# A shifted DMA copy and one mask in the decoding of the second layer's weights, with a load two steps sooner

## The chip, the cores and the metric

The kernel runs on one core of a Trainium2 chip. The metric is the device time of one execution in microseconds (us): the median of three runs. The profile is that of one further execution, whose own time stands beside its span.

## The reference

```python
w = softmax over the 7 taps of weight[8, 7], one set per group of 24 channels
x = causal convolution of x[4, 4096, 192] with w, along the sequence
x = x.reshape(16384, 192)
g = np.maximum(x @ moe_w_in, 0.0) ** 2        # 192 x 2048
x = g @ moe_w_out                             # 2048 x 192
h = x @ moe2_w_in
out = np.maximum(0.01 * h, h) @ moe2_w_out
```

The weights of both layers are float64. In DRAM each value is two 32-bit words, and the kernel decodes them on the chip.

## The kernel before

**Tiles and steps.** Tokens go in 32 tiles of 512. Each layer has 2048 hidden channels, which are handled in eight pieces p = 0 to 7 of 256; a unit (layer, tile) takes eight steps, one per piece. In a step PE computes the piece's hidden values of one tile (`g1`: h, nine rounds of products) and, two steps behind (LAG), adds the products with w_out of an earlier piece into the output banks (`g2` for the first two tiles, which are worked as a pair; `g2_one` with `paired` for all others). ACT takes h through the activation and rounds it to its high part (hi), the DVE subtracts to get the low part (lo). Steps 0 to 15 are the pair (1,0), (1,1); steps 16 to 23 are (1,2); 24 to 31 (1,3); from 32 on come (2,0), (2,1) and so on. Layer 2's piece p is first used in step 32 + p.

**Weights.** `load_w` (L166 to L172) issues five DMAs on SP per piece. Loads are numbered 0 to 15: load 8 + p is layer 2's piece p. The tile of 128 x 768 pairs of words stands in a place that is lent to it until its own weights come there (`lent`), or in a stage tile "w" or "y". `decode` makes the high and the low part of a piece p in steps on the DVE, some handed to ACT:

- mantissa: m = the high word's lowest 9 bits (L234); rest: the low word times 2^-32 plus m, written over the low word (L250). Together they are the fraction below the high part.
- exponent: t = the high word's exponent and upper mantissa bits (L266), and on ACT a relu that rescales it (L269).
- sign: puts the sign into t (L281); then four DMA copies on SP put the high parts where the products read them (L287).
- power: p = t's power of two (L296); low: low word times p times a power of two (L302, three instructions of one or two blocks).

**What sets the order.** The scheduler keeps the program's order on each engine. In steps 0 to 15 a hand-written string per step (ROW, played by `play`) says what comes when: d the next decode operation, L the next load, p a part of the convolution, a letter each for activation, square, high and low part. From step 16 on `single` and `fill` choose by a model of the engines' times (`clock`, `on`): a decode operation is placed if its gate allows it and if the model says that the step's own chain still ends in time. A load is issued after the low part of the piece whose place it takes (AFTER).

**POOL.** Its queue holds the casts of x by DMA, the accumulating copies of layer 1's decoding (L245), the later `differences` (L149, L151), and one more thing: where two halves of the PE array change over on an output bank, PE's new product depends on an empty instruction on POOL, which depends on PE's last product of the other half. For `g2` these are the 16 at L670, for `paired` those at L718:

```python
                if holder.get((u, k), half) != half:
                    done = nc.gpsimd.nop(nofuse=True).ins
                    tc.add_manual_dep(done, lastly[u, k].name, in_turn, reason="halves take turns on a bank")
                    tc.add_manual_dep(ins, done.name, in_turn, reason="halves take turns on a bank")
```

Of the kernel before, what the change touches and what calls it, by code (L numbers as in the profile page):

```python
# [8 lines left out]

F32 = mybir.dt.float32  # L10
F32R = mybir.dt.float32r
I32 = mybir.dt.int32
U32 = mybir.dt.uint32
ACTF = mybir.ActivationFunctionType
ALU = mybir.AluOpType
# [3 lines left out]
P = 128  # L19
TT = 512  # L20
# [16 lines left out]
BY_DMA = 3  # L37
ADD = 3
CAST = ((1, 2), (1, 3))
ASIDE = (2, 3, 4)  # L40

# [9 lines left out]
    "AdbaBwyddwHdp",  # L53
    "ddgAbpdahllB",
    "ybpdwLAyBdpawThrp",
    "ldppABabhlp",
    "AyBydpabhdww",
    "lyAdappLhlBdwp",
    "pAbpayhBrbywd",
    "wddBAlahlrdb",  # L60
)
# [5 lines left out]
def conv_moe_moe2_kernel(  # L67
# [10 lines left out]
    nc = tc.nc  # L78
    B, S, D = x.shape
# [4 lines left out]
    NP = NF // 2  # L84
# [6 lines left out]
    NW = NI + NO  # L91

    const = ctx.enter_context(tc.tile_pool(name="const", bufs=1))
    stage = ctx.enter_context(tc.tile_pool(name="stage", bufs=1))
# [9 lines left out]
    f32 = lambda ap: ap.bitcast(F32)  # L104
# [9 lines left out]
    WIDE = NI + 21 * R  # L114
# [44 lines left out]
    ring = const.tile([P, 3, TT], F32, name="ring")  # L159

    def load_w(l, p, t):
# [9 lines left out]
        nc.sync.dma_start(out=to[:, :, 2 * R:], in_=src[:, :, 0:2 * P])  # L171
        nc.sync.dma_start(out=to[:, :, 0:2 * R], in_=src[:, :, 2 * P:])  # L172

    held, holding = deque(), [False]
    ready, owner_m, raised_at, signed = {}, {}, {}, {}

    clock = {"D": 0, "A": 0}
# [22 lines left out]
    def decode(l, p, t, a, b):  # L200

        lo_w, hi_w = t[:, a:b, 0], t[:, a:b, 1]
        n = b - a
        one, two = 160 + n * 52 // 100, 170 + n * 104 // 100
# [17 lines left out]
            lows.append((lambda s: s[:, NO - a:], z[:, WI_LO:WI_LO + NI]))  # L222
        T = {}
        by_add = l == 1 and p >= ADD

        def mantissa():
            if by_add and p % 2:
# [26 lines left out]
        def exponent():  # L254
            release()
            if l == 1 and p > 0:
                if "t" not in words:
                    words["t"] = lent(0)
                T["t"] = words["t"][:, p % 2 * NW:(p % 2 + 1) * NW]
            elif l == 2 and p in ASIDE:  # L260
                if "t2" not in words:
                    words["t2"] = stage.tile([P, NW, 2], I32, tag="y", name="t2").rearrange("p n w -> p (n w)")
                T["t"] = words["t2"][:, p % 2 * NW:(p % 2 + 1) * NW]
            else:
                T["t"] = stage.tile([P, NW], I32, tag="t", name="t")[:, 0:n]
            nc.vector.tensor_scalar(out=T["t"], in0=hi_w, scalar1=0x7FFFFE00, scalar2=None, op0=ALU.bitwise_and)  # L266

            def relu():
                nc.scalar.activation(out=T["t"], in_=T["t"], func=ACTF.Relu, scale=8.0, bias=bias_e)  # L269
                raised_at[l, p] = max(clock["A"], clock["D"] + AFTER_D) + 870 + AFTER_A  # L270

            on_scalar(relu, 850)
# [19 lines left out]
        def power():  # L292
            if not (l == 1 and p > 0):
                owner_m["m"] = 0
            T["p"] = stage.tile([P, NW], I32, tag="t" if l == 1 and p > 0 else "m", name="p")[:, 0:n]
            nc.vector.tensor_scalar(out=T["p"], in0=T["t"], scalar1=-(2 ** 23), scalar2=None, op0=ALU.bitwise_and)  # L296

        def low_():
            assert not by_add or "added" in T
            ready[l, p, 1] = True  # L300
            for of, to in lows:
                nc.vector.scalar_tensor_tensor(  # L302
                    out=to, in0=of(T["r"]) if by_add else f32(of(lo_w)), scalar=2.0 ** -20, in1=f32(of(T["p"])), op0=ALU.mult, op1=ALU.mult
                )

        return [(one, mantissa), (two, rest)], [(one, exponent)], [(two, sign), (one, power), (two, low_)]


    phases = [[(1, 0), (1, 1)], [(1, 2)], [(1, 3)], [(2, 0)], [(2, 1)], [(2, 2)], [(2, 3)]]
# [531 lines left out]
    def evac(u):  # L841

        l, q = u
        o = ops.pop(u)
        tags.extend(tag_of[u][k] for k in ((0, "m"), (1, "m"), (0, "r"), (1, "r")))
        T = [2 * q, 2 * q + 1]
        z = {}

        def take(i):
            z[i] = ring[:, i, :]  # L850
            (nc.vector.tensor_copy if i else nc.scalar.copy)(out=z[i], in_=o[i, "m"])

        def shift(i):
            if i == 0:
                z["s"], z["r"] = f32(stage.tile([P, NW], I32, tag="m", name="zs")[:, 0:TT]), ring[:, 2, :]
            nc.scalar.copy(out=z["s"][halves(i)], in_=o[i, "r"][halves(1 - i)])

        def add(i):
            v = halves(i)
            nc.vector.tensor_add(out=z["r"][v], in0=o[i, "r"][v], in1=z["s"][v])  # L860

        now = [lambda: take(0), lambda: take(1), lambda: shift(0), lambda: add(0), lambda: shift(1), lambda: add(1)]
        if l == 1:
            then = []
            for i in range(2):
                b, a = splits((2, T[i]), lambda i=i: z[i], lambda: z["r"])
                then += [p + ((2, T[i]),) for p in ((a[0], b[0], a[1], b[1]) if i else a + b)]
            return now, then

        y = y_of(2 * q)  # L870

        def main(i):
            nc.vector.transpose(out=y()[:, i], in_=z[i])
            for j in range(4):
                store(y(), i, j, T[i], 32 * j)

        def rest():
            nc.vector.transpose(out=y()[:, 2], in_=z["r"])
            for j in range(4):
                store(y(), 2, j, T[j // 2], P + 32 * (j % 2))  # L880

        return now, [(700, lambda: main(0), None, None), (700, lambda: main(1), None, None), (700, rest, None, None)]

    with tc.manual_schedule():
# [7 lines left out]
        def load(n):  # L892
            if n >= len(loads):
                return
            l, p = loads[n]
            since[n] = now[0]
            if n < NP or NP + 1 < n < 2 * NP - 1:
                t = lent(n if n < NP else n + 1 - NP).rearrange("p (c w) -> p c w", w=2)
            else:
                t = stage.tile([P, NW, 2], I32, tag="w" if n == NP + 1 else "y", name="w")  # L900
            load_w(l, p, t)
            words[n] = t

        def fill_dec():
            parts = [(0, NO, NW), (0, 0, NO)] + [(n, 0, NW) for n in range(1, len(loads))]
# [7 lines left out]
            def stage_(j, k):  # L913
                if j >= len(parts):
                    return
                n, a, b = parts[j]
                cost = {0: (780, 1180), 1: (620,), 2: (1230, 580, 1260)}
                l, p = loads[n]
                need = first_use["w", l, p] - LEAD_W - (((2 if p >= ADD else 3), 1, 0) if l == 1 else (4, 2, 1))[k]
                for m, c in enumerate(cost[k]):  # L920
                    def run(j=j, k=k, m=m, n=n):
                        if j not in got:
                            begin(j)
                        got[j][k][m][1]()
                    run.second = (k, m) in ((0, 1), (2, 2))
                    gate = (lambda n=n: now[0] >= since[n] + 2) if k == 0 and m == 0 else None
                    if l == 2 and (k, m) == (2, 0):
                        gate = lambda p=p: (2, p) in raised_at and raised_at[2, p] <= clock["D"]
                    if l == 2 and k == 1 and p:
                        at_ = p - 2 if p in ASIDE[1:] else ASIDE[0] - 1 if p == ASIDE[-1] + 1 else p - 1  # L930
                        gate = lambda at_=at_: (p == ASIDE[0] or signed[2, at_] + 5000 <= clock["D"]) and not (
                            SECOND <= now[0] < THIRD and now[0] % NP == NP - 1
                        )
                    dec.append((need + (LATE and l == 1 and p >= ADD and (k, m) == (2, 2)) + (l == 2 and k == 2 and m > 0), c, run, gate))
                if k == 2 and a == 0:
                    if n in AFTER:
                        dec.append((need, 0, lambda n=n: load(AFTER[n]), None))

            stage_(0, 1)
            stage_(0, 0)  # L940
            for j in range(len(parts)):
                if parts[j][0] == NP - 1 or j == 0:
                    stage_(j, 2)
                    stage_(j + 1, 0)
                    stage_(j + 1, 1)
                else:
                    stage_(j + 1, 0)
                    early = j + 1 < len(parts) and parts[j + 1][0] - NP in ASIDE + (ASIDE[-1] + 1,)
                    if early:
                        stage_(j + 1, 1)  # L950
                    stage_(j, 2)
                    if not early:
                        stage_(j + 1, 1)
            for k in range(len(dec) - 2, -1, -1):
                dec[k] = (min(dec[k][0], dec[k + 1][0]),) + dec[k][1:]
            for k, z in enumerate(dec):
# [285 lines left out]
        for s in range(NS):  # L1242
# [62 lines left out]
                    decode_one()  # L1305
            begun += length(s - 1)
            if s == 2 * NP:
                clock["D"] = clock["A"] = begun + 2500
            if late:
                if late[0] not in hi:  # L1310
# [48 lines left out]
```

## Time and profile before

| | |
|---|---|
| median of three runs | 2041.4 us (2041.13 to 2041.49) |
| profiled execution | 2040.87 us |
| its span | 2039.2 us |
| granted TensorE clock | 1.0 |
| busy: PE, PEld, DVE, ACT, POOL | 2030.6, 1964.9, 1698.7, 1458.2, 42.2 us |

The span is what the trace covers; the execution's own time is 1.7 us longer. PE is TensorE's matmuls and PEld its weight loads. A releaser in square brackets is the instruction whose end let the waiting engine go on. An engine's name with a q (POOLq, SPq) is its queue: there stand the waits, DMA issues and empty instructions, which are not counted as busy.

### The profile page before, as it was taken

How to read it: one execution, taken by the hardware profiler on the slowest of the kernel's cores; microseconds unless marked ns; L12 is line 12 of the kernel's file. 1: busy time of each engine (PE TensorE's matmuls, PEld its weight loads, DVE VectorE, ACT ScalarE, POOL GpSimd, SP SyncE). 2: the span in 40 equal slices, each digit the busy share in tenths (PEclk: the TensorE clock that was granted, in tenths of full speed). 3: DMA queues.
4: the chain of work that ended last, by engine and by line, in shares of the span. 5: the costliest groups of instructions: out<-in, count | busy, mean ns of one | idle time of the engine just before them, and what ended most of it. 6: DMA issues, size and time to landing. Idle time of an engine off the chain costs nothing.

```text
span 2039.2 us, 47094 instructions
## 1 busy us (share of the span) xinstructions
PE 2030.6 (100%) x18552; PEld 1964.9 (96%) x18552; DVE 1698.7 (83%) x2656; ACT 1458.2 (72%) x2638; POOL 42.2 (2%) x82
## 2 busy tenths in 40 slices
PE   9999999999999999999999999999999999999998
PEld 5999999999999999999999999999999999999998
DVE  8899878788887978879788897888878888798775
ACT  7897567676676866767677676766767667687675
POOL 1004010000000000000000000000000000000000
PEclk9999999999999999999999999999999999999999
DMA  8662121222212212131211212122122221221111
GB/s 189 146 160 75 25 45 27 49 30 49 38 27 52 37 44 36 30 60 30 48 26 39 52 27 48 29 50 38 27 49 30 49 38 27 52 35 42 24 30 27
DMA packets 240087, 98.66 MB, mean 48 GB/s; under 512 B 208568, under 2 KB 225080, under 8 KB 239864
## 3 DMA queue, kind: packets, MB, share of 16 engines
q1 hardware_dynamic: 236696, 92.54, 22.7%
q0 software_dynamic: 1168, 2.75, 0.7%
q8 instruction: 145, 2.38, 0.5%
q14 instruction: 78, 0.64, 0.1%
q10 hardware_dynamic: 2000, 0.36, 0.1%
HBM read 25.19 MB, written 12.58 MB: 19 GB/s over the span
## 4 chain that ended last, share of the span: by engine, by line
PE 98%; ACT 1%; DVE 0%; DMA 0%; issue 0%; POOL 0%; DVEq 0%; ACTq 0%; POOLq 0%
PE h L556 48%; PE o1m L556 16%; PE o1r L556 16%; PE o0m L556 8%; PE o0r L556 8%; PE conv L460 1%; PE idle_o L1003 0%; ACT g L588 0%; DMA w<-lent 0%; ACT g L597 0%; ACT hi L615 0%; DVE lo L619 0%; DVE w L302 0%; ACT x L487 0%; ACT ring L241 0%
## 5 line engine op out<-in xcount | busy, mean ns | idle before, releaser
L556 PE MATMUL h<-x,w 64*128 64x512 f32 x9216 | 1350.9, 376 | 0.5 <-DMA w<-lent 0.4
L556 PEld LDWEIGHTS h<-x,w 64*128 64x128 f32 x9216 | 1061.5, 186 | 7.3 <-ACT hi L615 0.8
L619 DVE TENSOR_TENSOR lo<-g,hi 128x512 fp32r<-128x512 f32 x1022 | 665.6, 689 | 266.2 <-ACT hi L615 250.6
L556 PE MATMUL o1m<-hi,w 64*128 64x512 f32 x2044 | 613.8, 378 | 0.3 <-ACT ring L755 0.3
L615 ACT CAST hi<-g 128x512 fp32r<-128x512 f32 x1020 | 586.1, 621 | 22.9 <-DVE g L595 12.9
L556 PE MATMUL o1r<-hi,w 64*128 64x512 f32 x2012 | 601.0, 378 | 0.0
L590 ACT ACTIVATE g<-h 128x512 f32<-128x512 f32 x512 | 281.7, 596 | 308.3 <-PE h L556 308.3
L588 ACT ACTIVATE g<-h 128x512 f32<-128x512 f32 x512 | 282.8, 596 | 159.8 <-PE h L556 159.5
L556 PEld LDWEIGHTS o1m<-hi,w 64*128 64x128 f32 x2044 | 359.2, 186 | 20.8 <-ACT ring L755 0.7
L556 PE MATMUL o1r<-lo,w 64*128 64x512 f32 (+1 forms) x990 | 372.6, 376 | 0.0
L556 PEld LDWEIGHTS o1r<-hi,w 64*128 64x128 f32 x2012 | 352.9, 186 | 20.2 <-ACT ring L752 0.3
L556 PE MATMUL o1m<-both,w 64*128 64x512 f32 x958 | 360.6, 376 | 0.0
L631 DVE TENSOR_TENSOR both<-lo 128x512 fp32r<-128x512 f32 x479 | 331.6, 692 | 20.7
L556 PE MATMUL o0m<-hi,w 64*128 64x512 f32 x1056 | 314.8, 378 | 0.0
L556 PE MATMUL o0r<-hi,w 64*128 64x512 f32 x1020 | 307.5, 379 | 0.0
L556 PE MATMUL o0m<-lo,w 64*128 64x512 f32 x544 | 202.6, 377 | 0.0
L556 PE MATMUL o0r<-lo,w 64*128 64x512 f32 (+1 forms) x542 | 201.6, 376 | 0.0
L556 PEld LDWEIGHTS o0m<-hi,w 64*128 64x128 f32 x1056 | 186.6, 186 | 0.7
L597 ACT ACTIVATE g<-g 128x512 f32<-128x512 f32 x285 | 177.7, 632 | 7.4
L556 PEld LDWEIGHTS o1r<-lo,w 64*128 64x128 f32 (+1 forms) x990 | 182.6, 184 | 0.3
L556 PEld LDWEIGHTS o0r<-hi,w 64*128 64x128 f32 x1020 | 180.2, 186 | 1.1 <-POOLq L718 0.7
L556 PEld LDWEIGHTS o1m<-both,w 64*128 64x128 f32 x958 | 178.4, 186 | 0.5 <-DVE both L631 0.3
(129 smaller groups left out, 1288.0 us busy)
## 6 DMA issues: line engine op xcount, KB each, us to landing
x<-x SPq DMA_DIRECT2D x189, 256.0 KB
out_dram<-y SPq DMA_DIRECT2D x188, 64.0 KB
raw_a<-in_x_dram SPq DMA_DIRECT2D x127, 64.0 KB
raw_b<-in_x_dram SPq DMA_DIRECT2D x62, 64.0 KB
lent<-in_moe_w_out_dram SPq DMA_DIRECT2D x13, 256.0 KB
lent<-in_moe_w_in_dram SPq DMA_DIRECT2D x13, 192.0 KB
w<-t SPq DMA_DIRECT2D x8, 256.0 KB
lent<-in_moe_w_in_dram SPq DMA_DIRECT2D x13, 128.0 KB
```

The source lines that it names most:

```text
L460: nc.tensor.matmul(out=acc, lhsT=diag[k], rhs=src, start=(k == 0), stop=(k == K - 1))
L556: return nc.tensor.matmul(out=o.rearrange("p (b a) -> p b a", a=2), lhsT=w, rhs=z.rearrange("p (a b) -> p b a", a=2), start=begin, stop=end_,)
L588: nc.scalar.activation(out=g, in_=hps.pop((u, f)), func=ACTF.Relu)
L590: nc.scalar.activation(out=g, in_=hps.pop((u, f)), func=ACTF.Prelu, alpha=0.01)
L597: nc.scalar.activation(out=g, in_=g, func=ACTF.Square)
L615: nc.scalar.copy(out=a, in_=gsp[u, f])
L619: nc.vector.tensor_sub(out=b, in0=gsp.pop((u, f)), in1=f32(hi[u, f]))
L631: nc.vector.tensor_add(out=c, in0=f32(lo[u, 2 * p]), in1=f32(lo[u, 2 * p + 1]))
```

## The change

For layer 2 mantissa and rest go. In their place POOL issues a DMA copy of the piece's whole tile, as 16-bit words and shifted by one of them (`shift`): at the low word's place in the copy there then stand the low word's upper half and the high word's lower half. One DVE operation (`mask`) keeps the lowest 25 bits of it and writes them over the low word; the later product with the power uses 2^-36 instead of 2^-20 and reads it as an integer. The power is written in place of the high word. The copy goes to a constant place ("w27", "w26"), to the stage tile "y", or into the place of the piece's own weights ("own"). Copies 0 and 1 are issued after the low part of layer 1's piece 7 (load 7), 2 and 3 after that of (2,0), 4 before the mask of (2,2), and 5, 6, 7 after the low parts of (2,4), (2,5), (2,6).

The load of (2,1) (the L of step 13's string) is played in step 11 and goes to a lent place instead of the stage tile "w". At step 16, where the model's clocks are set anew, the times that gates compare with are set anew with them.

```diff
-ASIDE = (2, 3, 4)
+MOVED = ("w27", "w26", "y", "w27", "y", "own", "own", "own")
+SHIFTED, LOADED = 6500, 6000
...
-    "ldppABabhlp",
+    "LldppABabhlp",
     "AyBydpabhdww",
-    "lyAdappLhlBdwp",
+    "lyAdapphlBdwp",
...
+    def shift(p):
+
+        t, how = words[NP + p], MOVED[p]
+        if how in "wy":
+            z = stage.tile([P, NW, 2], I32, tag=how, name="shifted")
+        else:
+            z = const.tile([P, WIDE], I32, tag=f"w2{p}" if how == "own" else how, name="shifted")[:, 0:2 * NW]
+            z = z.rearrange("p (c w) -> p c w", w=2)
+        flat = lambda y: y.rearrange("p c w -> p (c w)").bitcast(I16)
+        nc.gpsimd.dma_start(out=flat(z)[:, 0:4 * NW - 1], in_=flat(t)[:, 1:4 * NW])
+        shifted[p] = z
+        shifted_at[p] = max(clock["D"], clock["A"], loaded_at[p])
...
+        def mask():
+            T["r"] = t[:, a:b, 0]
+            nc.vector.tensor_scalar(out=T["r"], in0=shifted[p][:, :, 0], scalar1=2 ** 25 - 1, scalar2=None, op0=ALU.bitwise_and)
...
-            T["p"] = stage.tile([P, NW], I32, tag="t" if l == 1 and p > 0 else "m", name="p")[:, 0:n]
+            if moved:
+                T["p"] = t[:, a:b, 1]
+            else:
+                T["p"] = stage.tile([P, NW], I32, tag="t" if l == 1 and p > 0 else "m", name="p")[:, 0:n]
...
-        return [(one, mantissa), (two, rest)], [(one, exponent)], [(two, sign), (one, power), (two, low_)]
+        return [(one, mask)] if moved else [(one, mantissa), (two, rest)], [(one, exponent)], [(two, sign), (one, power), (two, low_)]
...
-            if n < NP or NP + 1 < n < 2 * NP - 1:
+            if n < NP or NP < n < 2 * NP - 1:
...
+                    if moved and k == 0:
+                        gate = lambda p=p: shifted_at[p] + SHIFTED <= clock["D"]
...
+                if moved and k == 0 and p == 2:
+                    dec.append((need, 0, lambda: shift(4), None))
                 if k == 2 and a == 0:
                     if n in AFTER:
                         dec.append((need, 0, lambda n=n: load(AFTER[n]), None))
+                    if n == NP - 1:
+                        dec.append((need, 0, lambda: (shift(0), shift(1)), None))
+                    if n == NP:
+                        dec.append((need, 0, lambda: (shift(2), shift(3)), None))
+                    if l == 2 and MOVED[p + 1:p + 2] == ("own",):
+                        dec.append((need, 0, lambda p=p: shift(p + 1), None))
...
             if s == 2 * NP:
+                for at_ in (raised_at, signed, shifted_at, loaded_at):
+                    at_.update({k: min(z - max(clock.values()), 0) + begun + 2500 for k, z in at_.items()})
                 clock["D"] = clock["A"] = begun + 2500
```

PE's order and ACT's instructions are the same in number and kind. How instructions move, on three engines (rows as the order listing prints them; empty instructions are not listed):

POOL, the part behind layer 1's decoding; before:

```order
29 L613 DMA hi<-g 128x512
30 L245 DMA ring<-lent 128x768
31 L487 DMA x<-acc_b 64x512 x2
32 L149 CAST w_1204<-w_1204 128x64
33 L151 TENSOR_TENSOR w_1204<-w_1204 128x64 x2
34 L149 CAST w_1314<-w_1314 128x64
35 L151 TENSOR_TENSOR w_1314<-w_1314 128x64 x2
```

Now:

```order
30 L267 DMA ring<-lent 128x768
31 L511 DMA x<-acc_b 64x512
32 L187 DMA shifted<-w 128x3071
33 L187 DMA shifted<-lent 128x3071 x3
34 L511 DMA x<-acc_b 64x512
35 L187 DMA shifted<-lent 128x3071 x3
36 L151 CAST w_1269<-w_1269 128x64
37 L153 TENSOR_TENSOR w_1269<-w_1269 128x64 x2
38 L187 DMA shifted<-w 128x3071
```

Eight copies are new (shifted): four stand between the two casts of x (x<-acc_b), three behind the second, and the last behind the first differences.

SP, around the load of (2,4), whose five rows end each piece; before (w_1314 is the place of (2,1)'s weights):

```order
95 L465 DMA x<-x 64x1024 x4
96 L287 DMA w_1314<-t 128x512
97 L287 DMA w_1314<-t 128x128
98 L287 DMA w_1314<-t 128x2x64
99 L287 DMA w_1314<-t 128x64
100 L465 DMA x<-x 64x1024 x2
101 L403 DMA raw_a<-in_x_dram 32x16x32 x4
102 L166 DMA lent<-in_moe_w_in_dram 64x3x256
103 L167 DMA lent<-in_moe_w_in_dram 64x2x256
104 L168 DMA lent<-in_moe_w_in_dram 64x256
105 L171 DMA lent<-in_moe_w_out_dram 128x2x256
106 L172 DMA lent<-in_moe_w_out_dram 128x2x128
```

Now (w_1316 is that place):

```order
95 L307 DMA w_1316<-t 128x512
96 L307 DMA w_1316<-t 128x128
97 L307 DMA w_1316<-t 128x2x64
98 L307 DMA w_1316<-t 128x64
99 L489 DMA x<-x 64x1024 x3
100 L168 DMA lent<-in_moe_w_in_dram 64x3x256
101 L169 DMA lent<-in_moe_w_in_dram 64x2x256
102 L170 DMA lent<-in_moe_w_in_dram 64x256
103 L173 DMA lent<-in_moe_w_out_dram 128x2x256
104 L174 DMA lent<-in_moe_w_out_dram 128x2x128
```

The load came behind the high copies of (2,1), six copies of x and four loads of raw_a; now it comes behind the high copies and three copies of x.

DVE, from the last steps of the pair to the low part of (2,0); before:

```order
131 L234 TENSOR_SCALAR m<-w 128x768
132 L619 TENSOR_TENSOR lo<-g,hi 128x512 x2
133 L250 SCALAR_TENSOR_TENSOR w<-w,m 128x768
134 L619 TENSOR_TENSOR lo<-g,hi 128x512 x3
135 L851 COPY ring<-o1m 128x512
136 L860 TENSOR_TENSOR ring<-o1r,zs 64x512
137 L860 TENSOR_TENSOR ring<-o0r,zs 64x512
138 L281 SCALAR_TENSOR_TENSOR t<-w,t 128x768
139 L619 TENSOR_TENSOR lo<-g,hi 128x512 x2
140 L296 TENSOR_SCALAR p<-t 128x768
141 L302 SCALAR_TENSOR_TENSOR w_1204<-w,p 128x2x192
142 L302 SCALAR_TENSOR_TENSOR w_1204<-w,p 128x64
```

Now:

```order
126 L286 TENSOR_SCALAR t<-w 128x768
127 L643 TENSOR_TENSOR lo<-g,hi 128x512
128 L246 TENSOR_SCALAR w<-shifted 128x768
129 L286 TENSOR_SCALAR t<-lent 128x768
130 L643 TENSOR_TENSOR lo<-g,hi 128x512 x2
131 L301 SCALAR_TENSOR_TENSOR t<-w,t 128x768
132 L643 TENSOR_TENSOR lo<-g,hi 128x512
133 L319 TENSOR_SCALAR w<-t 128x768
134 L325 SCALAR_TENSOR_TENSOR w_1269<-w 128x2x192
135 L325 SCALAR_TENSOR_TENSOR w_1269<-w 128x64
136 L325 SCALAR_TENSOR_TENSOR w_1269<-w 128x384
```

The sign and the low part of (2,0) stood behind the three evacuations of the pair's banks (ring), and now stand before them.

## Rows read from the trace of the kernel before

**Rows 1.** The page's head, its busy shares and its chain, whole span.

```profile
span 2039.2 us, 47094 instructions
...
PE 2030.6 (100%) x18552; PEld 1964.9 (96%) x18552; DVE 1698.7 (83%) x2656; ACT 1458.2 (72%) x2638; POOL 42.2 (2%) x82
...
PE 98%; ACT 1%; DVE 0%; DMA 0%; issue 0%; POOL 0%; DVEq 0%; ACTq 0%; POOLq 0%
```

**Rows 2.** The table of stretches: length, busy time (count) of each engine, PEclk, DMA share, GB/s.

```profile
88.78:189.01 100.23, 99.96 (x913) 94.69 (x911) 91.49 (x141) 83.78 (x152) 22.49 (x25) 1.00 0.43 113
...
500.00:1000.00 500.00, 500.00 (x4623) 489.20 (x4621) 419.21 (x655) 355.87 (x643) 0.00 (x0) 1.00 0.21 39
```

**Rows 3.** POOL's turns by line (count, ns, first to last), whole span and five narrow windows.

```profile
L718 POOLq EVENT_SEMAPHORE  x1488: 17/17/17, 100.5 to 2031.0; - x186
...
  PEld o0r L556: 0.7, 4
...
L670 POOLq EVENT_SEMAPHORE  x1: 17/17/17, 97.4 to 97.4; - x1
...
L718 POOLq EVENT_SEMAPHORE  x1: 17/17/17, 109.0 to 109.0; - x1
...
L718 POOLq EVENT_SEMAPHORE  x1: 17/17/17, 133.5 to 133.5; - x1
...
L718 POOLq EVENT_SEMAPHORE  x1: 17/17/17, 146.7 to 146.7; - x1
...
L718 POOLq EVENT_SEMAPHORE  x1: 17/17/17, 158.7 to 158.7; - x1
```

**Rows 4.** POOL's timeline, 60 to 120 us: start, length, line, operation [idle, releaser].

```profile
93.94 0.52 POOL L487 DMA_DIRECT2D x<-acc_b  x1 [24.24 <-PE o1r L556]
```

**Rows 5.** Groups of DVE instructions by line and form, 88.8 to 189 us.

```profile
L234 DVE TENSOR_SCALAR m<-lent 128x768 int32<-128x768 int32 x5 | 3.6, 720 | 0.1
...
L250 DVE SCALAR_TENSOR_TENSOR lent<-lent,m 128x768 f32<-128x768 uint32 x5 | 6.3, 1270 | 0.1
...
L266 DVE TENSOR_SCALAR t<-lent 128x768 int32<-128x768 int32 x5 | 3.4, 680 | 0.0
...
L281 DVE SCALAR_TENSOR_TENSOR t<-lent,t 128x768 int32<-128x768 int32 x5 | 6.0, 1207 | 0.0
...
L296 DVE TENSOR_SCALAR p<-t 128x768 int32<-128x768 int32 x8 | 4.7, 583 | 0.1
```

**Rows 6.** SP's timeline of DMA issues, 76 to 115 us.

```profile
82.95 0.63 SPq L166 DMA_DIRECT2D w<-in_moe_w_in_dram  x1
...
102.38 3.18 SPq L287 DMA_DIRECT2D w<-t  x4
...
108.91 5.39 SPq L465 DMA_DIRECT2D x<-x  x4
```

**Rows 7.** The page's DMA issues: KB each, us from issue to landing.

```profile
ring<-lent POOLq DMA_DIRECT2D x3, 384.0 KB, 4.7
...
x<-acc_b POOLq DMA_DIRECT2D x2, 128.0 KB, 2.7
```

**Rows 8.** ACT's timeline, 86 to 106 us.

```profile
89.95 0.62 ACT L615 CAST hi<-g 128x512 fp32r<-128x512 f32 x1
```

**Rows 9.** DVE's timeline, 86 to 110 and 128 to 160 us.

```profile
90.41 0.72 DVE L234 TENSOR_SCALAR m<-w 128x768 int32<-128x768 int32 x1 [0.78 <-DMA w<-in_moe_w_out_dram]
...
104.87 1.38 DVE L302 SCALAR_TENSOR_TENSOR w<-w,p 128x384 fp32r<-128x384 f32 x3
...
107.48 0.68 DVE L496 TENSOR_TENSOR x<-ring,x 128x512 fp32r<-128x512 f32 x1
...
130.92 1.29 DVE L619 TENSOR_TENSOR lo<-g,hi 128x512 fp32r<-128x512 f32 x2 [0.18 <-ACT hi L615]
...
144.65 1.27 DVE L619 TENSOR_TENSOR lo<-g,hi 128x512 fp32r<-128x512 f32 x2
...
156.92 1.27 DVE L619 TENSOR_TENSOR lo<-g,hi 128x512 fp32r<-128x512 f32 x2
```

More of the change, by code (lines that the diff above doesn't have):

```diff
@@ L11 @@
 F32R = mybir.dt.float32r
+I16 = mybir.dt.int16
 I32 = mybir.dt.int32
@@ L172, in load_w @@
         nc.sync.dma_start(out=to[:, :, 0:2 * R], in_=src[:, :, 2 * P:])
+    shifted, shifted_at, loaded_at = {}, {}, {}
+    def shift(p):
[9 more added lines that the diff above has]
+        shifted_at[p] = max(clock["D"], clock["A"], loaded_at[p])
     held, holding = deque(), [False]
@@ L224, in decode @@
         by_add = l == 1 and p >= ADD
+        moved = l == 2 and p < len(MOVED)
+        def mask():
+            T["r"] = t[:, a:b, 0]
+            nc.vector.tensor_scalar(out=T["r"], in0=shifted[p][:, :, 0], scalar1=2 ** 25 - 1, scalar2=None, op0=ALU.bitwise_and)
         def mantissa():
@@ L259, in exponent @@
                 T["t"] = words["t"][:, p % 2 * NW:(p % 2 + 1) * NW]
[L260 to L263, printed above, removed]
+            elif moved:
+                T["t"] = stage.tile([P, NW], I32, tag="tm"[p % 2], name="t")[:, 0:n]
             else:
@@ L302, in low_ @@
                 nc.vector.scalar_tensor_tensor(
-                    out=to, in0=of(T["r"]) if by_add else f32(of(lo_w)), scalar=2.0 ** -20, in1=f32(of(T["p"])), op0=ALU.mult, op1=ALU.mult
+                    out=to, in0=of(T["r"]) if by_add or moved else f32(of(lo_w)), scalar=2.0 ** (-36 if moved else -20),
+                    in1=f32(of(T["p"])), op0=ALU.mult, op1=ALU.mult
                 )
-        return [(one, mantissa), (two, rest)], [(one, exponent)], [(two, sign), (one, power), (two, low_)]
+        return [(one, mask)] if moved else [(one, mantissa), (two, rest)], [(one, exponent)], [(two, sign), (one, power), (two, low_)]
     phases = [[(1, 0), (1, 1)], [(1, 2)], [(1, 3)], [(2, 0)], [(2, 1)], [(2, 2)], [(2, 3)]]
@@ L854, in shift @@
             if i == 0:
-                z["s"], z["r"] = f32(stage.tile([P, NW], I32, tag="m", name="zs")[:, 0:TT]), ring[:, 2, :]
+                z["s"], z["r"] = f32(stage.tile([P, NW, 2], I32, tag="w", name="zs").rearrange("p n w -> p (n w)")[:, 0:TT]), ring[:, 2, :]
             nc.scalar.copy(out=z["s"][halves(i)], in_=o[i, "r"][halves(1 - i)])
@@ L896, in load @@
             since[n] = now[0]
-            if n < NP or NP + 1 < n < 2 * NP - 1:
+            if n < NP or NP < n < 2 * NP - 1:
                 t = lent(n if n < NP else n + 1 - NP).rearrange("p (c w) -> p c w", w=2)
             else:
-                t = stage.tile([P, NW, 2], I32, tag="w" if n == NP + 1 else "y", name="w")
+                t = stage.tile([P, NW, 2], I32, tag="y", name="w")
             load_w(l, p, t)
             words[n] = t
+            loaded_at[n - NP] = max(clock["D"], clock["A"]) + LOADED
         def fill_dec():
@@ L916, in stage_ @@
                 n, a, b = parts[j]
-                cost = {0: (780, 1180), 1: (620,), 2: (1230, 580, 1260)}
                 l, p = loads[n]
+                moved = l == 2 and p < len(MOVED)
+                cost = {0: (620,) if moved else (780, 1180), 1: (620,), 2: (1230, 580, 1260)}
                 need = first_use["w", l, p] - LEAD_W - (((2 if p >= ADD else 3), 1, 0) if l == 1 else (4, 2, 1))[k]
@@ L924, in run @@
                         got[j][k][m][1]()
-                    run.second = (k, m) in ((0, 1), (2, 2))
+                    run.second = (k, m) in ((0, 1), (2, 2)) and not moved
                     gate = (lambda n=n: now[0] >= since[n] + 2) if k == 0 and m == 0 else None
@@ L928, in stage_ @@
                         gate = lambda p=p: (2, p) in raised_at and raised_at[2, p] <= clock["D"]
-                    if l == 2 and k == 1 and p:
-                        at_ = p - 2 if p in ASIDE[1:] else ASIDE[0] - 1 if p == ASIDE[-1] + 1 else p - 1
-                        gate = lambda at_=at_: (p == ASIDE[0] or signed[2, at_] + 5000 <= clock["D"]) and not (
+                    if l == 2 and k == 1 and p > 1:
+                        at_ = p - 2 if p < len(MOVED) else p - 1 if p > len(MOVED) else len(MOVED) - 2 + len(MOVED) % 2
+                        gate = lambda at_=at_: signed[2, at_] + 5000 <= clock["D"] and not (
                             SECOND <= now[0] < THIRD and now[0] % NP == NP - 1
                         )
+                    if moved and k == 0:
+                        gate = lambda p=p: shifted_at[p] + SHIFTED <= clock["D"]
                     dec.append((need + (LATE and l == 1 and p >= ADD and (k, m) == (2, 2)) + (l == 2 and k == 2 and m > 0), c, run, gate))
+                if moved and k == 0 and p == 2:
+                    dec.append((need, 0, lambda: shift(4), None))
                 if k == 2 and a == 0:
@@ L941, in fill_dec @@
             for j in range(len(parts)):
-                if parts[j][0] == NP - 1 or j == 0:
+                n = parts[j][0]
+                if n == NP - 1:
+                    stage_(j, 2)
+                    stage_(j + 1, 1)
+                    stage_(j + 1, 0)
+                elif j == 0:
                     stage_(j, 2)
@@ L945, in fill_dec @@
                     stage_(j + 1, 1)
+                elif n < NP:
+                    stage_(j + 1, 0)
+                    stage_(j, 2)
+                    stage_(j + 1, 1)
+                elif n - NP + 1 < len(MOVED):
+                    stage_(j + 1, 1)
+                    stage_(j, 2)
+                    stage_(j + 1, 0)
                 else:
+                    stage_(j, 2)
                     stage_(j + 1, 0)
[L948 to L953, printed above, removed]
+                    stage_(j + 1, 1)
             for k in range(len(dec) - 2, -1, -1):
```

## Prediction

> **What bounds the kernel now.** I read the page's head, its busy shares and its chain first [rows 1]: TensorE is busy 2030.6 of 2039.2 us and carries 98% of the chain that ended last. So the time moves only where PE stands still, or stops standing still. PE's own instruction order is the same before and after (the order listings of PE differ in line numbers alone), so the question is what makes PE wait in the stretch that the change rewrites, from some 80 to 190 us.
>
> The table of stretches [rows 2] prices what can be gained there. In 500 to 1000 us, where nothing is decoded, 4623 matmuls take 500 us, 108.15 ns each. The stretch 88.78 to 189.01 has 913; at that price they take 98.7 us, and they take 100.2. **At most 1.5 us can be won**, however much the DVE is relieved. A measurement of this kernel tells about 0.2%, 4.1 us, from no change, so a measurable gain from this stretch is excluded by the row itself.
>
> What can be lost is larger, and the POOL rows show where. POOL is busy 42 us in all [rows 1], yet its in-order queue carries an empty instruction for each turn that two halves of the array take on a bank (the nops of `g2` and `paired`): PE's first product of the new half waits for it, and it waits for PE's last product of the old half. The trace has 1488 of one kind [rows 3], and PE did wait for some of them, 0.7 us in 4 waits. Among them stand those at 97.4, 109.0, 133.5, 146.7 and 158.7 us. The POOL timeline shows that the queue really stands at such turns: the cast of x at 93.94 had waited 24.24 us, and its releaser is a PE product [rows 4].
>
> **The change part by part.** *DVE.* Removed per piece: m, 0.72 us, and the rest, 1.27 us; added: one mask, a one-source operation on strided words like m, so about 0.7 us [rows 5]. That is 1.3 us off the DVE for each of eight pieces, some 10 us in all. Its cover: PE lost only 1.5 us here, so I take 1.0 us of gain, with bounds 0 and 1.5. The mask and the power now write every second word. The trace has such a write: the rest writes in place with that stride and takes 1.270 us where the sign, which reads as it does but writes densely, takes 1.207 [rows 5]; so I charge 0.06 us each, nothing on the path. The Trainium skill ("Vector Engine (DVE) Microarchitecture Reference", section on the SBUF access granule) says that a destination which hops every element runs at 1.71 ns a column. An estimate by that figure is 1.3 us for each mask and power, 0.6 to 0.7 us more than the rows; each of the three stalls C to E below would be about 1.3 us longer and the sum about 4 us larger. The row on the rest speaks against it, and the sum goes by the row.
>
> *ACT.* Its instructions stay the same in number; only relu moves. Nothing.
>
> *SP.* Same instructions. The load of (2,1) goes two steps sooner, past the four copies of (1,7)'s high parts: those copies are issued up to 3.2 us later (the five load issues behind the copies of 102.38 take from 105.56 to 108.91 [rows 6], about 3.2). They are first needed a step later; 0 to 1 us, I take 0.
>
> *Model's times.* They move gates and so the order on DVE; what it does is in the order listing already, and no instruction is added.
>
> *POOL.* Eight copies are added, each of 128 x 6142 bytes, twice the 384 KB of the accumulating copy, which lands 4.7 us after issue [rows 7]; bounds for one: 4.7 us, and 9.4 us if time goes by bytes. Every copy waits in POOL's queue for its source to be loaded, or for the piece whose place it takes over to be through its low part. **A turn that stands behind it in the queue waits too, and with it PE.** The order listing leaves the empty instructions out; which turn comes next behind which copy follows from the order of the calls in the program. The ready times are worked out from rows. Copies 0 and 1 wait for nothing late. Five of the other waits are late:
>
> A. Copies 2 and 3 stand before the turn of 97.4 us. Copy 3 reads the load of (2,3), which SP issues only after the high copies of (2,0), and these wait for the sign of (2,0). The sign now comes straight after the lo's of the last pair step; the hi they need starts at 89.95 [rows 8] and ends 0.62 later, two lo's end at 91.7, a sign takes 1.2 [rows 5]: 93 us. The high copies are issued in 3.2 us, the five parts of the load in 3.2 [rows 6]. Landing: the load first issued at 82.95 had landed when the DVE took it at 90.41 [rows 6, 9], 7.5 us later; the lower bound is 3.2 us of issuing and 2.7 us of the shortest copy [rows 7], 5.9. So the copy is ready at 102 to 104, and its issue takes 0.5 [rows 4]: the turn comes 5 to 7 us late. If signs and copies run faster than this, 3.5. I take 5.5; bounds 3.5 and 8.
>
> B. Copy 4 stands before the turn of 109.0 us. It reads the load of (2,4), which in SP's queue now stands behind the high copies of (2,1) and three copies of x, of which two wait for the split of ring. That split started at 107.48 [rows 9] and is tied to PE's evacuation; after it come two copies of x, 1.0 us, so the load starts at about 110 and lands at 115.9 to 117.5 on a clock that PE's earlier stall has already moved. That is 6.9 to 8.5 us late, less what the DVE and SP catch up while PE stands in A, for which I take 1 (no row shows it). I take 6; bounds 4.5 and 8.
>
> C, D, E. Copies 5, 6 and 7 wait for the low parts of (2,4), (2,5) and (2,6). In the changed order each low part stands behind a pair of lo's and the exponent, sign and power. C: the lo's start at 130.92 [rows 9] and end at 132.2; exponent 0.68, sign 1.21, power 0.58 [rows 5], low 1.4 (like 104.87 [rows 9]): 136.1, and 0.5 of issue, for the turn of 133.5: 3 us late. D: with the DVE 1.3 us ahead the first lo can start about 1 us before 144.65 [rows 9]; lo, mask, exponent, lo, sign, power and low take 5.2: 148.8, and 0.5, for the turn of 146.7: 2.5. E: the lo's of 156.92 [rows 9] can start 1 us sooner and end at 157.2; sign, power and low: 160.4, and 0.5, for 158.7; POOL's own differences of (2,0) stand there too: 3. Bounds for each: 1 and 4 (E: 5).
>
> Turns later than 158.7 us have no copy ahead of them. **Sum:** 5.5 + 6 + 3 + 2.5 + 3 - 1.0 = 19.0 us. Against the profiled execution's 2040.87 us that is 2059.9; the median of the runs stands 0.5 us above that execution, so **2060.4 us** in its terms. With all bounds: 2041.4 + 11 - 1.5 = 2050.9, and 2041.4 + 29 + 1 = 2071.4.
>
> **The rivals.**
> 1. *The copies cost their issue alone* (not slower). The copies' waits end before the turns need the queue. That decides once the sign of (2,0) and its load together come 5 us sooner than in A, and the low parts 3 us sooner than in C to E. Then each copy takes the 0.5 us of its issue [rows 4], hidden between turns, and the time is 2041.4 less 0 to 1.5: 2040.7. For it: POOL is idle 98% of the span [rows 1]. Against it: the times above have 4 to 8 us at A and B, and rows 4 show the queue waiting where a wait stands. The Trainium skill ("DMA: Bandwidth & Descriptors", "Issuing engines are not separate DMA queues") says that issuing on several engines saves only the sequencer's time of issuing, which is usually small; read as a price of eight issues on an idle engine, that gives this rival's time. Chance 0.06.
> 2. *Only A and B hold PE.* The DVE, with 1.3 us less per piece, brings the low parts forward and C to E vanish: 5.5 + 6 - 1 = 10.5, 2051.9 us. For it: C to E are late by no more than 3 us, and each is a sum of seven or eight terms. Against it: the lo's ahead are tied to hi's, and so to PE, and no work between them and the low parts can be left out. Chance 0.22.
> 3. *All five hold* (the forecast): 2060.4. Chance 0.55.
> 4. *The copies are slow*, 9.4 us and more, as two-byte shifted starts and twice the bytes might make them. Then the masks wait as well, lo's stand behind them on the DVE, and A, D and E grow by some 3 us each: 2069 and above. Nothing in the trace shows such a copy. Chance 0.12.
> 5. *The change doesn't do what it says*: the masks would not replace the two operations everywhere. The order listing shows all eight masks, so this, with all else, gets 0.05, spread like rivals 1 and 4.
>
> **How the numbers follow.** The likeliest is case 3, 2060.4. The range takes in case 2 with about 5 us below it and most of case 4: 2047 to 2069; it leaves out rival 1 and the upper part of rival 4, some 0.15. Faster by more than 0.2% needs 4.1 us, and the rows offer 1.5: 0.01. Within 0.2%: rival 1 and a little of the rest, 0.06. Slower: 0.93.
>
> **What would show it.** In the profile after: PE's span between 97 and 160 us has five gaps, with POOL's turns as releasers; POOL's timeline shows the shift copies with idle before them, released by loads (A, B) and by the DVE's low parts (C, D, E); DVE's busy time is down by about 10 us; the stretch from 500 us on is unchanged. One gap missing takes its term out. If there are no gaps while copies wait, the mechanism is wrong; if the gaps stand at the DVE's masks, rival 4 holds; if PE waits for lo's instead, I have mistaken the place of the loss.

## The result, and the profile after

The change makes the kernel slower: 2069.9 us (median of four runs, 2068.7 to 2070.3) against 2041.3 (four runs), a ratio of 1.0139 with a 95% interval of 1.0122 to 1.0157. Forecast were 2060.4 us, 2047 to 2069. The direction and the five places were right; the size lies 0.9 us outside the range.

The page of the changed kernel, its head, busy shares and chain (as in [rows 1]):

```profile
span 2068.1 us, 47110 instructions
...
PE 2040.2 (99%) x18552; PEld 1966.8 (95%) x18552; DVE 1688.7 (82%) x2648; ACT 1458.3 (71%) x2638; POOL 45.0 (2%) x90
...
PE 93%; DVE 2%; DMA 2%; SPq 2%; issue 1%; ACT 0%; POOL 0%; POOLq 0%; DVEq 0%
```

The span grew by 28.9 us and DVE's busy time fell by 10.0, from 1698.7, as the eight masks promised. PE's busy time grew by 9.6 us for the same 18552 matmuls: part of the loss is not standing still but running slower. The chain, 98% PE before, now goes through DMA, SP and DVE for some 6%.

PE's waits in the changed kernel (total, times, longest), then the same for three narrow windows, those of the turns B, C and D (115 to 128, 150 to 157 and 168 to 173 us):

```profile
PE o1m L580 <- POOLq L742: 9.6, 2, 7.7
...
PE o1r L580 <- POOLq L742: 4.8, 2, 2.6
...
PE o0m L580 <- POOLq L694: 2.6, 1, 2.6
...
PE h L580 <- DMA x<-x: 1.8, 1, 1.8
```

```profile
PE o1m L580 <- POOLq L742: 7.7, 1, 7.7
```

```profile
PE o1r L580 <- POOLq L742: 2.3, 1, 2.3
```

```profile
PE o1m L580 <- POOLq L742: 1.9, 1, 1.9
```

The five turns forecast to be late are late: A 2.6 us (the row of L694, where L670 was), B 7.7, C 2.3, D 1.9, and E the other 2.6 of the o1r row (its longest). That is 17.1 us. A sixth wait of 1.8 us, on a copy of x, was not in the forecast. POOL's timeline shows what the turns stood behind:

```profile
98.02 0.53 POOL L187 DMA_DIRECT2D shifted<-lent  x1 [13.95 <-DMA w<-t]
...
104.26 0.53 POOL L187 DMA_DIRECT2D shifted<-lent  x1 [5.71 <-DMA lent<-in_moe_w_out_dram]
...
125.64 0.56 POOL L187 DMA_DIRECT2D shifted<-lent  x1 [20.33 <-DMA lent<-in_moe_w_out_dram]
...
154.82 0.53 POOL L187 DMA_DIRECT2D shifted<-lent  x1 [28.63 <-DVE w L325]
...
171.65 0.53 POOL L187 DMA_DIRECT2D shifted<-lent  x1 [16.30 <-DVE w L325]
...
186.39 0.57 POOL L187 DMA_DIRECT2D shifted<-w  x1 [1.32 <-DVE w L325]
```

These are the copies 2 to 7, each with the wait in front of it: copy 2 is released by SP's high copies, 3 and 4 by the landing of a load, 5 to 7 by a low part of the DVE. PE takes up work within 0.1 us of the start of each of the last four issues (B to E). At A a cast of x stands between copy 3 and the turn; it is issued at 104.78, straight behind copy 3, and PE goes on at 104.81.

The table of stretches (PEclk, the granted clock, is the third number from the end, before DMA share and GB/s) for slices after the holds, and for 500 to 1000 us, which answers to [rows 2]:

```profile
92.00:96.00 4.00, 2.60 (x18) 2.21 (x20) 3.43 (x7) 3.04 (x7) 0.00 (x0) 0.85 0.28 92
...
96.00:100.00 4.00, 4.00 (x30) 3.63 (x28) 1.64 (x3) 2.87 (x6) 0.53 (x1) 0.72 0.58 175
...
104.00:108.00 4.00, 3.19 (x16) 2.49 (x18) 0.94 (x2) 1.43 (x3) 1.05 (x2) 0.63 0.66 228
...
124.00:128.00 4.00, 2.30 (x12) 1.84 (x14) 0.00 (x0) 0.00 (x0) 0.56 (x1) 0.50 0.98 269
...
128.00:132.00 4.00, 4.00 (x36) 3.47 (x34) 0.00 (x0) 2.64 (x5) 0.00 (x0) 0.88 0.66 181
...
154.00:158.00 4.00, 3.13 (x21) 2.88 (x23) 3.77 (x7) 1.39 (x3) 0.53 (x1) 0.78 1.06 318
...
158.00:162.00 4.00, 4.00 (x32) 3.76 (x30) 1.04 (x3) 3.26 (x6) 0.00 (x0) 0.79 1.11 261
...
170.00:174.00 4.00, 2.29 (x22) 2.03 (x24) 3.76 (x8) 2.25 (x5) 0.53 (x1) 1.00 0.62 225
...
186.00:190.00 4.00, 3.56 (x20) 3.30 (x22) 2.49 (x5) 1.33 (x3) 2.30 (x4) 0.62 0.84 286
...
500.00:1000.00 500.00, 500.00 (x4624) 489.08 (x4622) 418.50 (x655) 355.59 (x642) 0.00 (x0) 1.00 0.21 39
```

After the wait on x and after each hold but the one of D (170 to 174) the granted clock is down for 3 to 8 us, to 0.5 where it is lowest, the lower of its two levels. The time lost by that is the share that is missing times the slice's length, for 124 to 128 the 2.3 us in which PE was busy: 0.6 + 1.1 + 1.5 + 1.2 + 0.5 + 0.9 + 0.8 + 1.5 = 8.1 us. Of these 0.6 + 1.1 follow the wait on x, and 1.5, 1.6, 1.7 and 1.5 the holds A, B, C and E. Waits at turns 17.1, the wait on x 1.8 and the clock 8.1 make 27.0 of the 28.9 us; the other 2 us are short stops around the holds and the edges of the slow stretches, which I don't attribute. From 500 to 1000 us nothing changed.

What a product costs at either clock is seen on PE's timeline behind the wait on x:

```profile
93.40 1.56 PE L580 MATMUL h<-x,w 64*128 64x512 f32 x11 [1.84 <-DMA x<-x]
...
94.80 0.59 PE L580 MATMUL o1m<-hi,w 64*128 64x512 f32 x1
...
95.61 0.63 PE L580 MATMUL o1m<-lo,w 64*128 64x512 f32 x1
...
98.42 0.38 PE L580 MATMUL o0m<-lo,w 64*128 64x512 f32 x1
```

The first row resumes at the upper level; 1.4 us later the products get slower (0.59, then 0.63 us), and from 98.4 on they take 0.38 again.

### The profile page after: what moved, and what is told of

Its sections match the earlier page's. It is cut to its first block, busy times and chain, and to the rows that moved or that the text cites. A ratio compares the mean times of both kernels' runs of the same rounds, so it can differ in the third digit from the quotient of the medians.

```text
span 2068.1 us, 47110 instructions
## 1 busy us (share of the span) xinstructions
PE 2040.2 (99%) x18552; PEld 1966.8 (95%) x18552; DVE 1688.7 (82%) x2648; ACT 1458.3 (71%) x2638; POOL 45.0 (2%) x90
## 4 chain that ended last, share of the span: by engine, by line
PE 93%; DVE 2%; DMA 2%; SPq 2%; issue 1%; ACT 0%; POOL 0%; POOLq 0%; DVEq 0%
PE h L580 46%; PE o1m L580 16%; PE o1r L580 16%; PE o0m L580 8%; PE o0r L580 8%; DMA lent<-in_moe_w_out_dram 1%; SPq L307 0%; DVE lo L643 0%; DMA x<-x 0%; DMA lent<-in_moe_w_in_dram 0%; DVE acc_b L471 0%; SPq L168 0%; SPq L169 0%; DVE lent L301 0%; SPq L173 0%
```

## The experiments

Two theories stood against each other. Theory 1: a copy that waits in POOL's queue holds the turns behind it, and each hold lets the clock fall. Theory 2: the copies' bytes, or the DVE's new order, hold PE wherever the copies stand.

**The wait without the change.** To the kernel before, two copies of one word per partition are added (e3), each behind the issue of a load and waiting for it:

```diff
+        probe = const.tile([P, 2], I32, name="probe")
...
+                    if n in (8, 9):
+                        dec.append((need, 0, lambda n=n: nc.gpsimd.dma_start(out=probe[:, n - 8:n - 7], in_=words[n + 3][:, NO, 0:1]), None))
```

> The kernel before, with two copies of one word per partition added on POOL's queue, each behind the issue of a load, (2,3) and (2,4), and waiting for it to land. No traffic, no other order on DVE, ACT or SP. Theory 1: the turns behind them wait for the landing: the load of (2,3) is issued from 105.7 and lands at 111.6 to 113, so the turn of 109.0 comes 2.5 to 4 us late, the other load's likewise, and after each the clock is down for some 3 us (1.5 us lost): 2046 to 2053 us. Theory 2: copies of 512 bytes cost nothing, 2041 to 2042.

The control (e8) has the same two copies, but they read the load before, `words[n + 2]`, which has landed:

> As e3_probe_before, but each of the two copies of one word reads the tile of the load before, which has landed by then. Theory 1: a copy that needn't wait holds no turn but for its issue of 0.6 us: 2041 to 2042 us, no wait of PE for L718 above 0.6. If a copy on POOL's queue costs a turn by being there (descriptors made by POOL): 2043 or more.

Measured: e3 2056.9 us against 2040.8 (ratio 1.0078, 1.0063 to 1.0093); e8 2040.7 against 2041.1 (0.9997, 0.9988 to 1.0007). The waits of PE and POOL's timeline in e3:

```profile
PE o1r L556 <- POOLq L718: 11.6, 2, 6.4
```

```profile
110.47 0.58 POOL L940 DMA_DIRECT2D probe<-lent  x1 [15.57 <-DMA lent<-in_moe_w_in_dram]
...
136.13 0.55 POOL L940 DMA_DIRECT2D probe<-lent  x1 [25.09 <-DMA lent<-in_moe_w_in_dram]
```

and POOL's timeline in e8:

```profile
103.05 0.57 POOL L940 DMA_DIRECT2D probe<-lent  x1 [7.51 <-PE o0m L556]
...
119.87 0.55 POOL L940 DMA_DIRECT2D probe<-lent  x1 [16.25 <-PE o0m L556]
```

Two copies of 512 bytes cost 16 us when they wait, and nothing that can be measured when they don't. In e8 their releaser is a product of PE, that is, the turn ahead of them in the queue: they found their data ready. So it is the wait in the queue and neither the traffic nor the presence of a copy. The holds are 5.2 and 6.4 us, 11.6 together; of the other 4.5 us most is the clock again, as the slices behind the two holds show:

```profile
108.00:112.00 4.00, 1.48 (x8) 1.20 (x10) 2.50 (x4) 0.00 (x0) 0.58 (x1) 0.58 0.89 240
...
112.00:116.00 4.00, 4.00 (x24) 3.22 (x22) 0.00 (x0) 0.81 (x2) 0.00 (x0) 0.56 0.19 61
...
136.00:140.00 4.00, 3.82 (x20) 3.13 (x22) 0.00 (x0) 0.00 (x0) 0.55 (x1) 0.58 0.60 119
```

By the reckoning used above (the first slice by the 1.48 us in which PE was busy) that is 0.6 + 1.8 + 1.7 = 4.1 us. The time came out above what was expected (2046 to 2053), since both holds lasted longer than the 2.5 to 4 us estimated for each and the clock was charged too low, with 1.5 us a hold.

**The change without the waits.** In e1 the copies 2 to 7 are put on a list and issued in a later step, when load and place are ready:

```diff
+    def shift_ready(s):
+        while waiting and s >= waiting[0][1] + 1 and NP + waiting[0][0] in since and s >= since[NP + waiting[0][0]] + 4:
+            shift(waiting.pop(0)[0])
...
-                        dec.append((need, 0, lambda: (shift(2), shift(3)), None))
+                        dec.append((need, 0, lambda: (ask(2), ask(3)), None))
...
             now[0] = s
+            shift_ready(s)
```

with the same for copies 4 to 7, and the mask of a piece due two steps later.

> The changed kernel, with the shift copies 2 to 7 issued later: each in the first step after the low part that makes its place free, and not before four steps after its load was issued, so that POOL finds it ready. Theory 1 (a waiting copy in POOL's queue holds the turns of PE's halves, and each hold lets TensorE's clock fall for some 3 us more): PE's waits for POOL at L742 and L694 go from 17 us to under 3, the clock stays at its upper level but for the wait on the copy of x at 91 us, which stays (1.8 us and its share of the clock): 2042 to 2047 us. Theory 2 (the copies' bytes, or the DVE's new order, hold PE wherever the copies stand): 2060 us or more.

Measured: 2050.3 us (ratio 1.0045, 1.0029 to 1.0062), 19.6 less than the change. PE's list of waits has no turn of POOL left; at its head stands

```profile
PE o1m L592 <- DVE lo L655: 4.6, 3, 4.0
```

and the DVE's timeline gives the cause:

```profile
129.19 0.56 DVE L298 TENSOR_SCALAR t<-lent 128x768 int32<-128x768 int32 x1 [5.05 <-DMA w<-t]
```

An exponent stood 5.05 us on the DVE for SP's high copies of an earlier piece, which read the t it writes over, and lo's stood behind it. Theory 1's own claim, that the holds go, came true; the time lies 3 us above its range for a new wait that the later order made. Theory 2 had 2060 or more.

**The same with the new wait removed.** e6 lets an exponent go 9 us after that sign, where it was 5; e5 does so too and decodes only pieces 0 to 4 from copies.

```diff
-                        gate = lambda at_=at_: signed[2, at_] + 5000 <= clock["D"] and not (
+                        gate = lambda at_=at_: signed[2, at_] + 9000 <= clock["D"] and not (
```

> As e5_copies_later_five with all eight pieces from shifted copies. Theory 1: the 5.9 us at steps 24 to 26 go, the lo's behind the last pieces' decoding at step 35 stay late: 2042 to 2046 us. Rival: 2048 or more.

> As e1_copies_later, with only the pieces 0 to 4 decoded from a shifted copy (5 to 7 by mantissa and rest as before), and with an exponent let go 9 us of the model's time after the sign whose t it writes over, where it was 5: in e1 the DVE stood 5.05 us there for SP's high copies. Theory 1 (nothing is left but the waits that the profile of e1 names): the 5.9 us at steps 24 to 26 and the 1.4 us at step 35 go, 2041.5 to 2044 us. Rival (the copies' traffic costs PE something of its own): 2046 or more.

Measured: e6 2044.7 us (1.0022, 1.0012 to 1.0031), e5 2045.2 (1.0022, 1.0013 to 1.0031). e6 is where theory 1 put it; e5 is 1 us above its range, and of its remaining waits a copy of x (0.9 us) and sums of lo's around step 35 (0.7 us) are not in the kernel before, so its expectation that these go too was wrong. Whether the pieces 5 to 7 come from copies or not makes no measurable difference between the two.

**The wait on the copy of x.** The load of (2,1) two steps sooner pushes it back in SP's queue; but copies 0 and 1 move data at the same time. e7 makes the early load alone in the kernel before; e2 is e1 with the load back in step 13, and also with copy 1 put on the list, so it moves two things; e9 is e6 with copy 1 issued in step 15.

```diff
-    "ldppABabhlp",
+    "LldppABabhlp",
...
-    "lyAdappLhlBdwp",
+    "lyAdapphlBdwp",
...
-            if n < NP or NP + 1 < n < 2 * NP - 1:
+            if n < NP or NP < n < 2 * NP - 1:
```

> The kernel before with the one change that the load of (2,1) is played in step 11 and goes to a lent place. If the order of SP's queue makes PE wait for the copy of x at step 16: a wait of 0.5 to 2 us there, 2042 to 2045 us. If it takes the traffic of copies 0 and 1 besides: 2041 us, no such wait.

> As e1_copies_later, and the load of (2,1) back in step 13, where it stood before; copy 1 is issued when that load is there. Theory 1 with the load as the cause of the wait on the copy of x (SP issues that copy 3.6 us later than before, since the load stands in front of it): that wait goes too, 2039 to 2042 us. If the traffic of copies 0 and 1 is its cause, it stays in part: 2043 to 2046. Theory 2: 2060 or more.

> As e6_copies_later_eight, with copy 1 issued in step 15 and not beside copy 0, so that one copy's traffic and not two stands ahead of the copy of x that PE needs at step 16. If the traffic of copies 0 and 1 makes PE wait there (0.7 us in e6, 1.8 us in the changed kernel): the wait is under 0.3 us, 2041.5 to 2044 us. If not, the wait stays and the time is that of e6, 2044 to 2046.

Measured: e7 2040.7 us against 2041.1 (0.9999, 0.9989 to 1.0008), no wait on x; e2 2047.4 (1.0034, 1.0021 to 1.0047), no wait on x either, but waits of PE for lo's, 3.4 us more than in the kernel before, with an exponent waiting on the DVE as in e1, so its range was missed; e9 2043.1 (1.0014, 1.0005 to 1.0023), no wait on x. SP's timeline, e7 and the changed kernel:

```profile
84.24 0.51 SPq L465 DMA_DIRECT2D x<-x  x1
```

```profile
86.01 0.51 SPq L489 DMA_DIRECT2D x<-x  x1
```

In e7 the copy of x is issued at 84.24, 1.8 us later than in the kernel before (82.40), and PE doesn't wait. With the copies 0 and 1 beside it, it is issued at 86.01 and PE stands till 93.40. In 88 to 92 us the DMA engines are busy in the changed kernel and all but idle in e7 (the number before the last is their share):

```profile
88.00:92.00 4.00, 3.56 (x33) 2.98 (x29) 2.58 (x4) 3.90 (x8) 0.00 (x0) 1.00 0.99 309
```

```profile
88.00:92.00 4.00, 4.00 (x42) 3.82 (x39) 3.54 (x6) 3.94 (x7) 0.00 (x0) 1.00 0.01 2
```

With copy 1 moved away the wait is gone (e9, with the load early as in the change). So the early load alone does not make the wait; it takes both copies, 768 KB each, in the same few us. Whether the two copies make it without the early load is open: no run has both copies and the load in its old place. In the runs with both copies in place the wait's length varies: 1.8 us in the changed kernel, 0.6 in e1, 0.8 in e4, 0.9 in e5, 0.7 in e6, 1.9 in e10.

**Two of the six copies.** e10 issues only copies 3 and 4 later, those that wait for loads, by the list of e1.

> The changed kernel with only copies 3 and 4, which wait for loads, issued later; copies 2 and 5 to 7 where the change has them. Theory 1: the holds at 101.9 and 117.6 us go with what the clock loses after them, 4.7 and 9.6 us by the lengths of their steps: 2053 to 2058 us, with three holds at turns left behind copies 5, 6 and 7, of 2 to 3 us each. If a hold that goes comes back at the next turn: 2062 or more.

Measured: 2057.1 us (1.0083, 1.0069 to 1.0097), inside the range; the four runs lie between 2055.1 and 2060.1, and the profile is that of the longest. PE's waits:

```profile
PE o1m L592 <- DVE lo L655: 4.8, 3, 4.3
...
PE o1m L592 <- POOLq L754: 3.5, 2, 1.9
...
PE o1r L592 <- POOLq L754: 2.5, 1, 2.5
...
PE h L592 <- DMA x<-x: 1.9, 1, 1.9
```

Three holds of 6.0 us in all are left (copies 5, 6, 7), and the exponent's wait of e1 is there too (4.8 us in the row of lo), so the agreement in time is partly made of a wait that the expectation didn't hold. A hold that goes does not come back at the next turn. Behind the wait on x, as long here as in the changed kernel, the clock did not fall:

```profile
92.00:96.00 4.00, 2.60 (x24) 2.31 (x25) 3.45 (x5) 3.01 (x7) 0.00 (x0) 1.00 0.26 90
```

**The model's times.** e4 leaves out the two lines that carry the times over at step 16.

> The changed kernel without the carrying over of the model's times at step 16. Theory 1: copies stand ahead of turns by their place in the program, whatever the gates say, but later masks move copies and low parts: 2055 to 2080 us, with waits on POOL's turns of 8 us or more in sum. If the carry-over is what puts the copies ahead of the turns, under 2050.

Measured: 2063.3 us in its one run. PE waits for POOL's turns 16.7 us in five waits, the longest 6.3:

```profile
PE o1m L580 <- POOLq L742: 9.0, 3, 6.3
...
PE o0m L580 <- POOLq L694: 6.1, 1, 6.1
...
PE o1r L580 <- POOLq L742: 1.6, 1, 1.6
```

So the holds are there without the carry-over too: it does not put the copies ahead of the turns. The change also sets the order of the decoding's steps anew in `fill_dec`, which the diff above leaves out; no run takes that alone back, but e9, which keeps it in the main, is 2.6 us above the kernel before.

## Why the prediction was right, and where it failed

- **What bounds the kernel, and the 1.5 us of possible gain**: not contradicted. DVE's 10 us less bought nothing: the best version without holds, e9, is 2043.1 us, 2.6 us above the runs of before on its chip. Half of that is one wait of PE at 171 us, where the last pieces' decoding now stands in front of lo's:

```profile
PE o1r L592 <- DVE lo L655: 1.3, 1, 1.3
```

No experiment points to a version faster than the kernel before. One row was read too far: the "0.7 us in 4 waits" of [rows 3] are waits of the weight loads (PEld), and PE's own waits in the kernel before hold no turn.
- **A to E, the turns held behind waiting copies**: right in all five places, and the mechanism is shown by e3 and e8 (the wait alone does it) and e1 (without it the holds go). In sum 17.1 us where 20.0 were forecast, and that they are so near is partly luck. A was 2.6 instead of 5.5, below its bounds of 3.5 to 8: copy 3 was issued at 104.3, about as worked out, but PE reached the turn over 4 us later than in the trace of before, since it had waited for x and then run at the lower clock. In e4, where the wait on x was 0.8 us and cost no clock, A's hold is 6.1. B was 7.7 instead of 6: the load of (2,4) went out from 118.3 and copy 4 followed at 125.6, and the 1 us of catching up that I took did not come. C, D and E were 2.3, 1.9 and 2.6 for 3, 2.5 and 3, inside their bounds. Two slips stand in their sums: the list for D adds up to 5.8 us by its own rows, not 5.2, and the 0.5 us of issue added at C, D and E did not come, since PE went on 0.05 us after the issue's start.
- **The step that failed: the sum had no term for the clock.** "Sum: 5.5 + 6 + 3 + 2.5 + 3 - 1.0" adds waits as if PE went on at its old pace after each. The rows show 6.4 us lost at the lower clock behind A, B, C and E, about 1.6 us each, and 1.7 behind the wait on x. e3 shows the same in another program: 4.1 us behind two holds. With the 6.4 us the sum of 19.0 would have been 25.4, or 2066.8 us, inside the range. The span grew by 9.9 us more than the sum. The 3.5 us that are not the 6.4 are made up of several: A, the wait on x and the clock behind it came to 6.1 where 5.5 stood for A; B was 1.7 above; C to E were 1.7 below; the gain of 1.0 did not come; and 1.9 are not attributed. The measured time lies inside "all bounds" (2071.4), but by a term that those bounds did not hold.
- **SP's price of "0 to 1 us, I take 0"**: wrong too. The copy of x came late, for 1.8 us and its share of the clock. I had counted the copies of high parts that SP issues later, and not that the copy of x moves data beside copies 0 and 1 (e7 and e9), for which I had written that they "wait for nothing late". What they make others wait for was not asked.
- **The strided writes**: charged 0.06 us each and nothing on the path. The groups of DVE instructions of the changed kernel:

```profile
L246 DVE TENSOR_SCALAR lent<-shifted 128x768 int32<-128x768 int32 x6 | 4.5, 749 | 0.0
...
L319 DVE TENSOR_SCALAR lent<-t 128x768 int32<-128x768 int32 x6 | 3.8, 640 | 0.2
```

The mask takes 0.749 us (m took 0.720) and the power 0.640 (0.583). The Trainium skill's figure for a destination that hops 4 KiB at every element ("Vector Engine (DVE) Microarchitecture Reference", the SBUF access granule), which the prediction gave without the 4 KiB, would by its estimate have made 1.3 us of either; the trace shows that it does not carry over to this step of two words.
- **Rival 4, slow copies**: out, though its "2069 and above" is the number nearest to the measured one. The masks don't wait (0.0 us of idle before them in the row above), and the copies land after 4.5 us by the median of six:

```profile
shifted<-lent POOLq DMA_DIRECT2D x6, 767.8 KB, 4.5
```

twice the bytes of the accumulating copy of [rows 7] in about its time, in spite of the start shifted by two bytes. All eight took 3.6 to 7.3 us.
- **Rivals 1 and 2**: out, since all five turns were late. The Trainium skill ("DMA: Bandwidth & Descriptors", "Issuing engines are not separate DMA queues") says that issuing on several engines saves only the sequencer's time of issuing. Read as the price of a copy, as rival 1 read it, this agrees with e8 (2040.7 against 2041.1), where the copies needn't wait; in e3 the same copies cost 16 us, because a copy that waits holds what stands behind it in the queue.

## What to carry to other kernels

An idle engine's queue is not free if another engine's turns pass through it: before an instruction that waits is put there, list what stands behind it, empty instructions too, and issue it only when its source is ready. Price a stall of TensorE with what comes after it: in the changed kernel each of five stops of 1.8 to 7.7 us cost another 1.5 to 1.7 us at the lower clock, and the sixth, of 1.9 us, nothing. And when work is taken off an engine, look first at how much PE loses to that engine; 1.5 us were to be had here, and 28.6 were paid for them.

## What was not expected of the hardware

- The clock's fall can come after the stop: behind the wait on x PE ran 1.4 us at the upper level before its products got slower, and was back 3.6 us after that; behind C and E it was much the same. Behind A and B the first products were slow already (0.57 us at 104.81, 0.79 at 125.70).
- Stops of 1.5 to 1.9 us went either way. The wait on x in the changed kernel (1.84 us) and the hold behind copy 7 in e10 (1.92) were followed by the lower clock. The hold of D (1.91), e10's wait on x (1.87, in the same place as that of the changed kernel), its hold behind copy 5 (1.62) and one of e4 (1.55) were not, nor were waits on x of 0.6 to 0.9 us. The stops of 2.3 us and more in these traces all were. What decides among the shorter ones stays open.
- e5 and e6 spread more than the kernel before (2043.9 to 2048.3 in ten runs each, e9 2042.8 to 2044.6). They have both copies beside the copy of x, e9 has not; that the wait on x and its clock make the spread is likely (the four runs above 2047.5 us have a granted clock of 0.998 or 0.999, the others 0.999 or 1.0), but it is not shown: no profile of a 2048 us run was taken.
